# A new order of the steps in a gated recurrence followed by a two-layer MLP

## The chip, the cores and the metric

One core of one Trainium2 chip. The metric is the device time of one execution in microseconds (us). Engines are named as in the profile: PE is TensorE (matmuls), PEld its weight loads, DVE is VectorE, ACT is ScalarE, POOL is GpSimd, SP is SyncE. Every DMA of this kernel is issued by SP ("SPq" in the profile), one after the other.

## The reference

For each of 4 batches and 8 heads (768 tokens, 48 dimensions) a state matrix of 48x48 is carried over the tokens, turned and damped by a complex gate per row; then the outputs of all heads make 3072 rows of 384, which go through a layer of 2048 features with a PReLU.

```python
mag = np.sqrt(a_re * a_re + a_im * a_im)
scale = np.minimum(mag, 0.999) / (mag + 1e-06)
a_re_n, a_im_n = (a_re * scale, a_im * scale)
for t in range(S):
    new_re = ar * S_re - ai * S_im
    new_im = ar * S_im + ai * S_re
    kv = np.einsum('bhd,bhe->bhde', k[:, :, t], v[:, :, t])
    S_re, S_im = (new_re + kv, new_im)
    y[:, :, t] = np.einsum('bhd,bhde->bhe', q[:, :, t], S_re)
...
h = x @ w_in
g = np.maximum(h, 0.0) + alpha * np.minimum(h, 0.0)
return (g @ w_out).astype(np.float32)
```

## The kernel before

**Tiling and stages.** The sequence is cut in chunks of 128 tokens: 4 batches of 6 chunks are 24 *units*. Nine *gate tasks* prepare the gates: three for the first batch (1, 2 and 3 chunks) and two of 3 chunks for each other batch. The work is written as Python generators, one per task; each `yield` ends a *step*, a few instructions on one engine.

- `gates` (L250 on) loads a_re and a_im into a gate buffer (tile gate, two of them in turn; GpSimd's memset L249 clears a last column), normalises the gate on ScalarE and VectorE (L253 to L301), builds products of magnitudes (L318; tile decs, stored by L323) and running products of phases. These are first products of eight neighbours (L338, L340, large ones on VectorE), then of the blocks (the same lines with 128x72 and 128x36 on GpSimd for all batches but the first), a short run over blocks (128x12, 128x6), a correction of the blocks (L396, L399), a renormalisation (L405 to L413), and the final large products on VectorE (L426, L429), which are stored by L421 and L431 (tile phs). ScalarE copies stand between (L366, L368). I call the stretch from the last large product of L340 to L413 GpSimd's chain of the task.
- `loads` brings q and k of a unit (tile KQ, L579, L581), its phases (tile PP, L587, called the rotation load) and its magnitudes (tile T, L594). `half_rows` (L560) copies values into a scratch in DRAM (vsc), `loads_v` brings values (tiles V and VL, L603 to L629).
- `unit` multiplies q and k by the phases (L661, L663), halves the chunk level by level (L717 on VectorE, copies L740 and L756 on ScalarE, sixteen small matmuls L678 on TensorE, masks L699 and L702), transposes k (L785), makes k times v (L797), sums the levels with the values (L817), updates the state (L826, L829 on VectorE) and takes its part of y (L841); ScalarE copies y out (L855), L860 stores it.
- `weights` brings the MLP's weights from 64-bit words to float32: ScalarE L507 to L511, GpSimd L515 (tile top), VectorE L517 and L519. `pieces` issues their loads and the small ones (start, L468; alpha, L471).
- `all_mlp` is the MLP over the finished rows: for each group of up to 256 rows (loaded by L873) and each of 16 blocks of 128 features, three matmuls (L889), ScalarE's relu of the negative part (L896), VectorE's alpha times it plus the input (L898; tile g_sb), and for each 128 rows one matmul into the output (L908), in 16 steps per output tile, copied by L918 and stored by L921.

**What sets the order.** Every instruction stands on its engine in the order in which it is emitted (`tc.manual_schedule()`); engines run their own lists in order, and wait for one another where data or a buffer asks for it. The order of emission is a string, ORDER, of 4292 letters (L30 to L72). Each letter names a task and lets it go one step on:

```python
    LETTERS = "ABCDEFGHIJKLMNOPQRSTUVWXYZabcdefghijklmnopqrstuvwxyz0123456789"
...
    def run(self, order):
        for c in order:
            next(self.tasks[self.LETTERS.index(c)], None)
```

A to I are the nine gate tasks; J is `loads`, K `half_rows`, L `loads_v`, M `pieces`, N and O the two `weights`, P to Z and a to m the 24 units, n `loads_x` and o the MLP. The names DVE, ACT, POOL, PE and DMA in the steps are functions that return nothing; the numbers in them have no effect here.

Of the kernel before, what the change touches and what calls it, by code (L numbers as in the profile page):

```python
# [27 lines left out]


ORDER = (  # L30
    "AAAAAAAAAAAAAAAABJJJJBBAAAAAAAAMMMMMAMAAAAAAAAAAALLLBBNNBBLABLAAALABALAAAANBNABBBBANAABABBANABOOAMBB"
    "OBBOAAAAAAKMAABBBABABABABABBAKKKKAALLKAABABABAABAABNAAAAABANBABALAAABAABNBNOBBBBOOOOBONBMNBNNBBBBNNJ"
    "OBOOOOOBBPBPCBNPCBBBBPCBBBBCCJJJOBBOBBKPPPPBCBBBBBMPNJJLNNBPNNBPBPBPBCNPBNCMBMCPPPPPJPCKKKKKKKKKKKKK"
    "BKBKPBBBMBCPBNOCNBOOBPCMNCLLCCBLPPPPPPPPPPPPPPPPCCMCBCCBKCCCPJOCOCDOJOCNNJCNNNNNCDCCKKKPCPCPPPPPPPPP"
    "CCQCOKOOOCMQCCQLDDDQCCLLLLLLJLLLLLLCLCCCJDJJJJJJJCCNJQQCDNCQCQCDDQQCDCCNNQCDDQQDDQCOCODDCDCDCCCQDDOQ"
    "CQOCQQQCDDDDKOCRQQCRQQQQQQCQQQRRRRQQQQQMnQCNDMCOCOOCDDDMCQCLQCLRCCCCRCRRLLLRCRRRoKJLQOOOOCoRoCoCRRCR"
    "oQQLLLLLoooKLLQLoQQQoQCoCDCooRooQoRRDooCCCCRRRRRRRRRRoCRCoCoCoCDoRQCJJJEooRRODooooNNNNNoEDRooRoRoooo"
    "RDnLLLLooOoOoOoRODLooRoLLLLLLRLLDNRNoLSoooooooooSoRRRRRooJJSooOoooooSoSSDSNDSSSESoooooooRoSNSSoooSDo"
    "ooSSSDJSJJEJJJJJJDoooooDoooEOSSSSooooSDoooSSSSSSooDDDDDDDooETTSSSEESooooSSSSSToSSEEESSooKSSSoSToJTTT"
    "ToooToooSToooTooSLoooToULoDLLoLDTJDDDDDDJTDoToEDTDDoDLDLoDDDDDDooLLLLLoToTLTooooooooooToTTTUTTToTooT"  # L40
    "ooTLJooDTTToooDUUTTTTTToULLLLULEEEEooEoTEoEDDDDDDDDDoDDEooooooUEToooUUUoooooonoUoEooJoUoooooUEUEDTDD"
    "DoTTUUUELEJULoooLLKLLLLKoUoooooDDooDDDJoKDKKoKoooUUUUUUooooDDDTTTTTToUoooUDUUUooooUooDUEDUUUUEUEEEoo"
    "EoEoooooooEoEEUooUooJooEoooUUUUoUUoFUUoooEEEoEoEooooooooooEEoEoEVFooFoJVVooJoFoJJnooooJJJJVJVFoLLooo"
    "oooooVVVFFLoLVoooooooooEEEEEEVoooVVVEEEEEEEEEEELEEEoEJJJooFoWWoEEoEEEVooooVVooVoooWJVVVVFLoooWooLooo"
    "oWVVVVVVWVWWJVoooVFFVooooXVWLoLLLVLLoLooKVKoEEEEWEVVVVVVVVVVVKLLWEEVoKooLLLLLooLXFWLVLLVLVLVVWWWWWoE"
    "EEEELooWooooEoEoEWEEEooJEWWWWWWWWEoooooooooJJEoEJEEEoooEWWWooooWoooWWWWWWWWWXLoooooWoFFFLXoLLXXXoXXo"
    "GLLWWooJoJLLXooXoXWWWWWWooooFoFFXXXXXXFoLooooLooFoXoFoFFFFFFFJJooFooonXoXXXXXGLLLLooFFXooooooXXXXooo"
    "XoXoFYFFFooooFoooFooXoFXXXXXXXXXFFXXXXXJJoYYJoooooLJLJFFFGoooFYLGFFFFFFFFooXoooYYYYYJYoYooXoooooooLo"
    "FFFFFoZZYYYYJooJYoYYZooooooYoooooZGoYYYYYYYYoYFLZZZZZZZFooooLoYYLFFLGFLLLLFLLooooYYoZZoYYYJYYYYJJLJJ"
    "LLGoFZZZLLFLLFLLLLFLooooLFFFFFFFFFFFooZZYooFFFFYZoGGGGFoooFYYYYYYYYZZZoooFooLooooFFFFFFZJFFFZooZZZZZ"  # L50
    "FZFoooooJZooZoZZnZZZZooZZZZZJZaZZLLFFJoLooooZZZJoooFoGaooGooaoaooooGGGLLLLLLLoLLLaaaaoooooooooaJaJaJ"
    "ooooooaGaaaaaoooHoooHoaaooooooGGoooaaGaaaGGaaaGGGooGGGooboaaaKboooooJooooooaooooaHGbGaGJGbJoaaGaabbb"
    "bJoJaaaaaabaaGLLbLLLoGoLGoLLLGaaHooHJooobboGoooooobboooGHobbbHobbooooJbooGHoJoboLHGJoooGbbbGbGbbbbJb"
    "ooocooooGoooJoonbooKoKGccoKKKKKooooooLbcccGcccooooHoooocooGoLLLbGJoJobbbobHbHGHHbbbLbHbGbbbbbLbbboGG"
    "GGGHoHoHoLoooGGGGGoGcGLcoGoGooGGGoGoGoGcGcGcccccLJoJoLooLoooLooooLLLcccLLccLdocoJocGcoGcGccGoocodooc"
    "oHHHddcHcccccccHdLcGGcGKoooLLHHGGHLoHLJLLHHoHooHooHooHdcGcdcdddcHcccooodoooGoooGGGGoGLLdLLLLLoGGGodd"
    "dddoooododoooonooooGooGodGddddooGdoddoooooooGHGddHoodJodHHHoJoJJJHHHJJJooooodooooooddddddddddddddddo"
    "HJeeooooJooooeoooooeoHooHHHHHHHdoLeeeooooooeeeeoefoofoooeeeoeoeooooJJooofLoooooLLooIeeofffeJeeooKooo"
    "oLLLLLLLLLHeeeeeeeeHHHHLooHoHoHoHeHoHeHooeeeeeeeeeeeeeeeJJIJJLLoHHeeHooHHIHfKHHfHHHHHoooHoJHoHooHffJ"
    "ooHoofgIooogoooofffILoHHoofffHoofofHHogHooooLnooooLLLooLoJoLgLHKLffffffffggoLIILggggfoooofKooooKHooL"  # L60
    "HooHgHooooHoHKKoKKHoofoIfKooofffoffffffffffLfJoJoofHfffHoooooHggggggoLLLLLooooIogoogIoooooHggIIIIooo"
    "ooooLgoggLgLLLILoooogggggoooIgILoooogggggggggggggJJJoohJJhhoLLIIJoooJJoggLgoooJooohhILLLoIoInoooLoho"
    "oiiJJhJohoLLJLLLhooooIIooooooooohhohhoIooooooihIhhhoIhhhoIIoIoIhIIIooiooooooooIIIihihhhhhhhooohLILIo"
    "oIooooIohooJJhJooohohoohhhhhIIIiIhIhhLhhhhLLoLooooiiiiooLoooLooooiiiooihohihhihooioioooooooJijJjiiJJ"
    "JIIIIIIIIIIIIIIIIIIIIIIIIIIooiooooIojooiooioioioooooiooooIIijIIIoIIoojjjjjILoIiiIoILoLILoLoLLLiijiij"
    "ioiLLLLLLLjjjLLLiLLoooIIIIIoooiooIIIIIiooooooooooooooijjjojojooLLoooooooojjjjijjjjIIiiiiooojoojooiii"
    "jjjIooJjjjjjjjjjjjjnjoJJJjjjjooooooooooooookooookokokooLoooLJJJJJJJooooooLookkooookkokokookookooookk"
    "kkkkkLLLooooooLLLLLLLoooookkkkoookkkkokooLookookkllokokkJkkkkkkkkkkkkkkololooooooooLLoooLooookLooLLL"
    "LllllllllLoLoooooooooJooooooooooooooooooooooonooooooooooooooooooJoooLLLollloooooooolllloooJooooooJJl"
    "loooooJLlllllllllooooooooololoolllllllllllllllllooooooomooooLoooomoooooooooomooooommmmmmomooooomoooo"  # L70
    "ooooLmmLmLLoooonooLomooooooooomLmmmLooooLLommmmmmmmoooooooomomomLLooooooooooomoooooooLomommmmmmmmmmm"
    "mmmomooooooooooooooooooooooooooooooooooooooooooooooooooooooooooooooooonooooooooooooooooooooooooooooo"  # L72
    "oooooooooooooooooooooooooooooooooooooooooooooooooooooooooooooooooooooooooooooooooooooooooooo")


# [925 lines left out]
```

## Time and profile before

| what | before |
|---|---|
| runs, us | 843.6, 840.4, 843.08 |
| median, us | 843.08 |
| span of the profiled execution, us | 845.2 |
| busy of the costliest line on TensorE (L889), us | 302.0 |
| the next (L908), us | 295.2 |
| costliest lines of VectorE (L717, L898), us | 148.5, 97.4 |
| bytes moved by DMA, MB | 130.91 |

The profile is of one execution, whose own time is its span of 845.2 us; it lies 2.1 us above the median of the runs. Busy time is the time in which an engine executed; the rest is waiting for another engine, a transfer or a buffer. A line of waits names the instruction that waited, who released it, and the time in total, the number of times and the longest. A line of the timeline names the start, the duration, the instruction with its tile shapes, and in brackets how long the engine stood idle before it and who ended that. "VectorE work ahead" of an instruction is the sum of the durations, in the profiled execution, of all VectorE instructions that stand in front of it in an order; it is a place in a list and not a time.

### The profile page before, as it was taken

The numbers are of one execution on the slowest core, as the hardware profiler recorded it, in microseconds if no ns is written. First come the engines' busy times: TensorE is split into PE (matmuls) and PEld (weight loads), VectorE is DVE, ScalarE is ACT, GpSimd is POOL, SyncE is SP. The second block draws the span as 40 slices with busy tenths as digits, with TensorE's granted clock in tenths as the row PEclk, the third lists the DMA queues.
The fourth block names the chain that finished last, engine by engine and source line by source line (L and its number), as shares of the span: only waits on it lengthen the run. The fifth ranks groups of instructions, "written<-read, shape, count | busy, mean of one in ns | idle before, by whom it ended". The sixth has DMA issues, their size and how long they took to land.

```text
span 845.2 us, 26866 instructions
## 1 busy us (share of the span) xinstructions
PE 699.6 (83%) x11488; PEld 529.6 (63%) x11488; DVE 653.3 (77%) x1020; ACT 443.3 (52%) x937; POOL 196.3 (23%) x293
## 2 busy tenths in 40 slices
PE   0002316688899999999999999999999999999998
PEld 0001315566777777767777777777676777777776
DVE  5999998689998999979998997687877656345212
ACT  7679686356745656665565634555444324233211
POOL 6241421126544411450115404300124000000000
PEclk9999997879999999999999999999999999999999
DMA  8496987675469677736965467747644482231100
GB/s 240 142 270 172 281 198 207 186 203 123 118 201 255 143 182 223 182 88 172 264 166 138 134 178 181 201 107 192 159 136 106 115 204 64 69 80 38 37 29 9
DMA packets 194174, 130.91 MB, mean 155 GB/s; under 512 B 74120, under 2 KB 185864, under 8 KB 194056
## 3 DMA queue, kind: packets, MB, share of 16 engines
q1 hardware_dynamic: 194056, 129.20, 59.2%
q8 instruction: 90, 1.47, 0.8%
q14 instruction: 28, 0.23, 0.1%
HBM read 100.82 MB, written 35.71 MB: 162 GB/s over the span
## 4 chain that ended last, share of the span: by engine, by line
PE 63%; DVE 17%; DMA 6%; issue 6%; ACT 5%; SPq 2%; POOL 0%; DVEq 0%; ACTq 0%; POOLq 0%
PE ps_o L908 25%; PE ps_h L889 25%; PE ps_lv L678 4%; DVE KQ L717 4%; PE ps_y L817 3%; PE ps_kv L797 2%; PE ps_y L841 2%; DVE gate L338 2%; DMA PP<-phs 2%; DMA phs<-gate 1%; DMA g_sb<-in_w_in_dram 1%; PE ps_kt L785 1%; DVE gate L426 1%; SPq L626 1%; DVE gate L340 1%
## 5 line engine op out<-in xcount | busy, mean ns | idle before, releaser
L889 PE MATMUL ps_h<-xT,w_in_sb 128*128 128x256 f32 (+1 forms) x1344 | 302.0, 356 | 2.9 <-DVE g_sb L898 1.6
L908 PE MATMUL ps_o<-w_out_sb,g_sb 128*128 128x384 f32 x768 | 295.2, 499 | 5.1 <-DVE g_sb L898 4.9
L889 PEld LDWEIGHTS ps_h<-xT,w_in_sb 128*128 128x128 f32 x1344 | 234.3, 193 | 74.1 <-issue 3.6
L898 DVE SCALAR_TENSOR_TENSOR g_sb<-g_sb,al,ps_h 128x256 f32<-128x256 f32 (+1 forms) x224 | 97.4, 437 | 115.5 <-ACT g_sb L896 115.1
L896 ACT ACTIVATE g_sb<-ps_h 128x256 f32<-128x256 f32 (+1 forms) x224 | 79.0, 353 | 204.2 <-PE ps_h L889 202.7
L908 PEld LDWEIGHTS ps_o<-w_out_sb,g_sb 128*128 128x128 f32 x768 | 138.0, 192 | 56.7 <-DVE g_sb L898 6.9
L717 DVE TENSOR_TENSOR KQ<-KQ,T 96x1024 f32<-96x1024 f32 x120 | 148.5, 1239 | 32.1 <-PE ps_lv L678 23.2
L678 PE MATMUL ps_lv<-WQ 96*32 96x32 f32 x2304 | 34.7, 204 | 79.0 <-DVE WQ L661 55.9
L678 PEld LDWEIGHTS ps_lv<-WQ 96*32 96x32 f32 x2304 | 26.6, 116 | 99.7 <-DVE WQ L661 56.1
L740 ACT COPY WQ<-KQ 96x1024 f32<-96x1024 f32 x48 | 50.0, 1041 | 27.8 <-DVE KQ L717 27.7
L338 POOL TENSOR_TENSOR gate<-gate 128x72 f32<-128x72 f32 x42 | 29.6, 704 | 125.6 <-ACT gate L368 122.8
L855 ACT COPY T<-ps_y 48x256 f32<-48x256 f32 x96 | 30.8, 364 | 51.8 <-PE ps_y L841 51.2
L338 DVE TENSOR_TENSOR gate<-gate 128x576 f32<-128x576 f32 (+5 forms) x84 | 50.0, 595 | 1.1
L515 POOL TENSOR_SCALAR top<-top 128x768 f32<-128x768 f32 x16 | 41.5, 2602 | 32.1 <-ACT top L507 32.1
L678 PE MATMUL ps_lv<-KQ,W 96*32 96x32 f32 x1536 | 25.2, 205 | 27.5 <-ACT W L756 23.2
L817 PE MATMUL ps_y<-A,VL 64*48 64x64 f32 x2304 | 42.4, 223 | 4.1 <-DMA VL<-vsc 2.5
L699 ACT ACTIVATE A<-ps_lv,columns 128x64 f32<-128x64 f32 x144 | 36.2, 336 | 17.2 <-PE ps_lv L678 17.1
L426 DVE TENSOR_TENSOR gate<-gate 128x1152 f32<-128x1152 f32 (+2 forms) x36 | 43.6, 1235 | 0.3
L756 ACT COPY W<-KQ 96x512 f32<-96x512 f32 x48 | 30.8, 642 | 23.9 <-DVE KQ L717 21.1
L817 PEld LDWEIGHTS ps_y<-A,VL 64*48 64x48 f32 x2304 | 39.8, 124 | 5.5 <-DMA VL<-vsc 2.7
L678 PEld LDWEIGHTS ps_lv<-KQ,W 96*32 96x32 f32 x1536 | 20.3, 115 | 29.6 <-ACT W L756 24.7
L785 PE MATMUL ps_kt<-ident,KQ 96*128 96x96 f32 x192 | 26.0, 260 | 15.4 <-DVE KQ L717 12.9
(106 smaller groups left out, 912.1 us busy)
## 6 DMA issues: line engine op xcount, KB each, us to landing
T<-decs SPq DMA_DIRECT2D x48, 384.0 KB
PP<-phs SPq DMA_DIRECT2D x24, 387.0 KB
KQ<-in_q_dram SPq DMA_DIRECT2D x48, 192.0 KB
decs<-gate SPq DMA_DIRECT2D x7, 1152.0 KB
phs<-gate SPq DMA_DIRECT2D x14, 576.0 KB
KQ<-in_k_dram SPq DMA_DIRECT2D x40, 192.0 KB
vsc<-in_v_dram SPq DMA_DIRECT2D x48, 144.0 KB
VL<-vsc SPq DMA_DIRECT2D x24, 288.0 KB
```

The costliest lines, as they stand in the source:

```text
L338: on(4 * k).tensor_tensor(out=m, in0=w[:, 1::-1].unsqueeze(2).to_broadcast([P, 2, 2, k]), in1=pairs_of(u), op=ALU.mult)
L426: TT(out=m[:, a], in0=U5[:, 1 + a], in1=turned(off3, o)[:, a].unsqueeze(1).unsqueeze(3).to_broadcast([P, L // 2, nb, 2]), op=ALU.mult)
L515: nc.gpsimd.tensor_scalar(out=top, in0=top, scalar1=F64_SMALL, scalar2=None, op0=ALU.max)
L678: nc.tensor.matmul(t[64 * i + j:64 * i + j + HC // 2, p], lhsT=keys(n, g), rhs=queries(n, g), start=True, stop=True)
L699: nc.scalar.activation(a[:, :, cols], t[:, :, at:at + name], AF.Copy, scale=s)
L717: nc.vector.tensor_tensor(out=x, in0=x if x0 is None else x0, in1=m, op=ALU.mult)
L740: nc.scalar.copy(z.rearrange("p i n t -> p i (n t)").rearrange("p i (m h) -> p m i h", h=h), bass.AP(tensor=KQ.tensor, offset=KQ.offset + ...
L817: nc.tensor.matmul(o, lhsT=Vp[h][64 * i:64 * i + 64, s, e_ * D:(e_ + 1) * D], rhs=a, start=False, stop=False)
L889: nc.tensor.matmul(p, lhsT=w_in_sb[:, f // 2, kk, f % 2 * P:(f % 2 + 1) * P], rhs=x_of[m][:, kk], start=(kk == 0), stop=(kk == NK - 1))
L896: nc.scalar.activation(gt, p, AF.Relu, scale=-1.0)
L898: nc.vector.scalar_tensor_tensor(out=gt, in0=gt, scalar=al_1[:, f:f + 1], in1=p, op0=ALU.mult, op1=ALU.add)
L908: nc.tensor.matmul(sums[0], lhsT=gt[:, c * P:(c + 1) * P], rhs=w_out_sb[:, f], start=(f == 0), stop=(f == NF - 1))
```

## The change

ORDER is another string with the same letters: each letter occurs as often as before, and so every task goes through the same steps, with the same instructions, shapes, engines and buffers. Only how the tasks are interleaved differs, from the 17th letter on. The heads of both strings, and the rest left out:

```diff
 ORDER = (
-    "AAAAAAAAAAAAAAAABJJJJBBAAAAAAAAMMMMMAMAAAAAAAAAAALLLBBNNBBLABLAAALABALAAAANBNABBBBANAABABBANABOOAMBB"
-    "OBBOAAAAAAKMAABBBABABABABABBAKKKKAALLKAABABABAABAABNAAAAABANBABALAAABAABNBNOBBBBOOOOBONBMNBNNBBBBNNJ"
...
+ORDER = (
+    "AAAAAAAAAAAAAAAAAAAAAAAAAAAMBMAMAJJBJJMBAAAAABAABALAAALAAAALABABAKKAKMKABKAAAMAAAAAAAAAAALABALAAAAAA"
...
```

Where some letters stand in the two strings (count of letters from 0; o is the MLP):

| letter | task | first, before | first, after | last, before | last, after |
|---|---|---|---|---|---|
| A | gate task, first chunk of batch 0 | 0 | 0 | 170 | 141 |
| B | gate task, chunks 1 and 2 of batch 0 | 16 | 28 | 355 | 261 |
| C | gate task, chunks 3 to 5 of batch 0 | 212 | 196 | 667 | 617 |
| D | gate task, first half of batch 1 | 366 | 299 | 1188 | 1150 |
| E | gate task, second half of batch 1 | 671 | 714 | 1555 | 1632 |
| I | gate task, second half of batch 3 | 2783 | 2674 | 3603 | 3524 |
| P | first unit | 209 | 191 | 399 | 503 |
| Q | second unit | 402 | 311 | 666 | 637 |
| X | ninth unit | 1425 | 1535 | 1790 | 1779 |
| b | thirteenth unit | 2156 | 2076 | 2396 | 2415 |
| j | twenty-first unit | 3393 | 3386 | 3628 | 3690 |
| m | last unit | 3955 | 3833 | 4104 | 4139 |
| o | the MLP | 580 | 529 | 4291 | 4291 |

More of the change, by code (lines that the diff above doesn't have):

```diff
@@ L30 @@
 ORDER = (
-    "AAAAAAAAAAAAAAAABJJJJBBAAAAAAAAMMMMMAMAAAAAAAAAAALLLBBNNBBLABLAAALABALAAAANBNABBBBANAABABBANABOOAMBB"
-    "OBBOAAAAAAKMAABBBABABABABABBAKKKKAALLKAABABABAABAABNAAAAABANBABALAAABAABNBNOBBBBOOOOBONBMNBNNBBBBNNJ"
-    "OBOOOOOBBPBPCBNPCBBBBPCBBBBCCJJJOBBOBBKPPPPBCBBBBBMPNJJLNNBPNNBPBPBPBCNPBNCMBMCPPPPPJPCKKKKKKKKKKKKK"
-    "BKBKPBBBMBCPBNOCNBOOBPCMNCLLCCBLPPPPPPPPPPPPPPPPCCMCBCCBKCCCPJOCOCDOJOCNNJCNNNNNCDCCKKKPCPCPPPPPPPPP"
-    "CCQCOKOOOCMQCCQLDDDQCCLLLLLLJLLLLLLCLCCCJDJJJJJJJCCNJQQCDNCQCQCDDQQCDCCNNQCDDQQDDQCOCODDCDCDCCCQDDOQ"
@@ L36 @@
[L36 to L70, printed above, removed]
@@ L71 @@
-    "ooooLmmLmLLoooonooLomooooooooomLmmmLooooLLommmmmmmmoooooooomomomLLooooooooooomoooooooLomommmmmmmmmmm"
-    "mmmomooooooooooooooooooooooooooooooooooooooooooooooooooooooooooooooooonooooooooooooooooooooooooooooo"
+    "AAAAAAAAAAAAAAAAAAAAAAAAAAAMBMAMAJJBJJMBAAAAABAABALAAALAAAALABABAKKAKMKABKAAAMAAAAAAAAAAALABALAAAAAA"
+    "BAABABBBABBBBAAAAOBBAABAABABOBNABAABABABAALBBJBNBKNBBBBNBBBBBBNOBBOBBNBBBBNBBNBBOBBBBOBNBLNPBBBBCBBC"
+    "BKNCBBPPBJBLPKJBBBBBCCBNBBBCCBBMBBMKJBBBMPBBBBNBCKBKBLPCNNPKLBJPCKPOPCOPPPOCCCCCOKJPPCCCLOCCJJCPCLJD"
@@ new lines @@
+    "DCNOJPCOPPCQJPDCJMMPCDPQLNCDOCLPPPKPCCKNNJCKPNPNCPPPPPOPKDPPPONPCPCQKCCOMQCCKPDCCNDNOPOCQCMDPOCQQPOM"
+    "CQCQPPOCDQQJCPCOCNQNCOQLLLLLLOQQCCOQOONCCDCCQQCCOJOCCKKQKLDRLQCQQCMDNQLQCPKQPDQDCDCLPPNCMLCDNNNLCQQL"
+    "NCDPCQQQQLMQJQCODQQJCNnQNCCCOoDLNROJCCCoQCLCoCQLLOOQONOOLMOCLCQCKCCRQoCCCRDoQLoRoooCCJooKCCoooooCoND"
+    "DCooooNoMoRoQRDoLCQOooooooRRoRLooQQQoQooRJooooNoONRoRoNNRoRoooNLoJooDRRoooOJJRLoooLoLLOJooooRSRNNJJR"
+    "oRooooRRoROoSJEDooooRoNRORoSREROONooRooSSSSnRSRRRRSRLOLRSDDDDESRoLDDoRooooRDoLLRoLLLLLRSoJRSRSJRoooo"
@@ new lines @@
+    "RSRooooSLoSoDSRoLLSooSDLSEoSSooSoooSDJoooJDoooDoDoSoSDoSSooTDSDEoSoTJDoKDKoToSSDoJDooSDEoDoSSSoTTDoE"
+    "SoJJSoDLLJLDToTooSTTEooTooDETSoSooSKKKoooToSDoEKSoSSoESoKoToEooTooSKKEETJoooLLoEoLooooJonTTLTDLoLooo"
+    "JoDDDDDDDDDDDDDDUToDoLDDLDooLoLDJDoUTDoTooDDDoJoEooToDDEooooDDoTDoDoDDoTTooEETDooTLDoDDTTTDoUoUooooD"
+    "TooooToTETDoDoDTTToLooDDLDoooEoooLLTLEUUoEUUoTooELDoLUEoUUTULLoLEJoTooToFETToUFEUoEUoJoEoUoUEUToUTEo"
+    "oooooToUoUoUTUEUoUooVLLUUUoEUooTooULUVoVUJoFUFUUEUJUULEFoVJUEUEULUUUJVooLUoEooVVEoUVUJJVoVooJEoEoooo"
@@ new lines @@
+    "oVoKoVVooVooVonLoVFEFLVooVoVLLooJVJooLELFEEJVooLELELWoEooLVWoKEEEoVWEVooEEFFEEooooVooVEVEWVoVoooLEoW"
+    "WWVVWooKoVoVKFoWoFVoVVVVVWFWVWLWVoVWVWLWFLoVVVJJVEJoEEKLVVoFWWoLEFoEoEEJEWEEVoFoEEEoooEEoEELWWEVoEWL"
+    "oEoLLFLWoooLWooLFoLoEWWoLWJWEooEooEXEEooWoooWJEEEoXJEFJEoJEEKoooXoEWoWoXFFooEoWWWoEFWFFoWXKLXFLoooFo"
+    "oEXoLooLLXXWoXWoLooXooooooFWXWoLELFLLLFoWFJWWLXWLoWXWXLXXoWXooWFoJXooooooooXFnFXXYFoJXXJoJXoXFJooXoX"
+    "FoYooFXoXoXoXooooooFoGGXXFXYXXXXJFFXXXoYLXXYXXFYYoJoFJYXoXoFoooooFYYZLoYGooooFoXooooooLYZJGYLJYGLLLL"
@@ new lines @@
+    "LYYZYYooYoooZooooooZJLoZLFFFFFFFFFFFFZJFFLFYFZLFFFLFJYoYYYGZYoZYoooYYYooYKFZJoooYoGoYYYGYYYGYYJFFFFY"
+    "FFFFLFoFFLYYZYZZLFFYYYYYYooFLFLJJoGJaoLGoFLFooZoFFoooFLLoFaZLooooooooooFZLLLLnZGGFZFooaooKFooooaoooo"
+    "GZJZJFZZaZZZaooFFFooZoFooZooooZoFoaZoZooZJZaaZZZJKZZaZZZZZZZZZaZZGooooooLLJGbJGooooooaaaaooGoooGoooo"
+    "oaoaoGHaooooaobooboGLHbLLboGLGoboLGoJoooooLoLoaLaabbbaooaLooLaaGboGoKbKbaooaaoooGaoGoaooLaaGHGbGGaab"
+    "aabaaGboaaaLLoaaaGbKooooGJJJoHbGoGbGaobGooHabooGooJooJGooJoGGGbbGbbobooHoLoJnoHHoJoooccooocooboobbbH"
@@ new lines @@
+    "HLoboooHoLoobooLobooLLLGGGbLoLLGoLGGGGLbGGGcGHHHbbHGbGbbLbbGGocGccbGGGGGGbcJcbHocGbboGoobGGoGcHoocoo"
+    "JoJbGGcHHLbcccHbooLoooHooLLdJdJcoooKoGooooooocGooodGocHGGGGodGooGooHGHoJodLGdGdcJccHcoocLHLLLLLcocGc"
+    "GGdooodoooodGLccLooJcoooocGoHocdGcHcHdcccccdHHHcLdHccdcccoGLooooGoodooLJdoooGHLoooLcoLGoooHLLLLLLdLc"
+    "odoooGoooooooooocoHcHdJddddoLdHooooHooHooooodoHJooodJeeooddodHoodooedddHHdIddddJeHJedJIdHKLeeedHdooL"
+    "LLHnHHHJddLLLdLoooeHeLLLHLdHHHooIooeoooHHLHHHHHHHooodeeeeeoeoedooooJJJooeooooeJeooIeoeeooIooooIoeeeI"
@@ new lines @@
+    "eoofHeooKooooeoefofLeoooHHHoooooefeeeefIIeefHeeIJeIfIHeIIeeJeeoooeJLoHoeLIofJfoLIooHHHLLJoIoHJoIoffI"
+    "LJgHHHLooooooooLoLfooooHogooHIoffffgIKnfIfooooHHLHHoLLooooogooooHoofLoHIHoooggffoffofoofooggoLJggooo"
+    "oHfHHHHooHHoofHooKoJHooooIooIooooHfffIoofoofoooIooHgfofffffgfLfIIIIKIgfgffffffggooIgogooLIoogoooIooo"
+    "ooIogIgKLgJfJIIIILIogofLooLIgggggIIIIILIIIoIJIIIoooooooooooogoKIgIoIooohJhhLoooIoLooooooLooJhooooIoh"
+    "LggoooLLhggJggJgJoIhhggLhgLggghhhghIgooooIooooooIoooooooooLJoLLIoighigooohhhJJhoohoooLLoohnhioiJKoIo"
@@ new lines @@
+    "oooohLJhIiLLhKohhhohhIKIIioooIIIIIooILIKIIIohiiiooJLhooohhLoooohJLiohhhihhhiihJoihhohijhhijIhhhiohhJ"
+    "IIooioooooooIooIJIIIIoooooooooIoooIIoooooLiLIJLLLLLLLLLLjoJoooooojooiojijIijiiojioiiojiIioIiooLijooj"
+    "oooooLiIiiiiijioiiLiLLjjIjoiiLJjijiioooooiiioooooojooooooooooooooooojJjjJJJnJooojjjjjjjoLLLoLookoooj"
+    "kjkokojoLojooooooooooooLLoLoLLjjjjjjjjjkkjjLjjLLLLjLLooLLooooLLoooooooojoooooooooJoooooojJjoJkoJookJ"
+    "ooJoJJkkokoooooooklklkolkokooklkooookooooolkkkLkLLlllkkkoJokkooooookoooookoooooooooooooookookokkklkk"
@@ L73 @@
+    "kLllllkkkollklkkJkJkookLoookkoolnmoLoooooooLoJJoooooooooooolooooooooLLooolLLLooooomooomLoomoooLLolLL"
+    "lmmllllolmooolomolmmmlloooooooooooooooooooooooooolooooooooolllmllllmllmlllLlLloolLoolomomommoLollmno"
+    "oooooooLooooommmoLmmooooooomooooooooooooooooooooLooLooooommmLmoooooooooooooooLLoooooLooooooooooooooo"
+    "ooooooooooooLmoomooomoooommmmmmmmmmmmmmmnooooooooooooooooooooooooooooooooooooooooooooooooooooooooooo"
     "oooooooooooooooooooooooooooooooooooooooooooooooooooooooooooooooooooooooooooooooooooooooooooo")
```

## The prediction

> **What bounds the kernel now.** I read the page's busy line first, then its 40 slices, then busy time by stretch, then the waits of VectorE, then single instructions of GpSimd. Columns of the first fence: busy time, share of the span; then a digit for each slice of 21.1 us.
>
> ```profile
> span 845.2 us, 26866 instructions
> PE 699.6 (83%) x11488; PEld 529.6 (63%) x11488; DVE 653.3 (77%) x1020; ACT 443.3 (52%) x937; POOL 196.3 (23%) x293
> PE   0002316688899999999999999999999999999998
> DVE  5999998689998999979998997687877656345212
> PEclk9999997879999999999999999999999999999999
> PE 63%; DVE 17%; DMA 6%; issue 6%; ACT 5%; SPq 2%; POOL 0%; DVEq 0%; ACTq 0%; POOLq 0%
> ```
>
> The two engines take turns: VectorE is nearly full for some 230 us while TensorE waits for it, then TensorE is full to the end (63% of the chain in the last line). Cutting the span there:
>
> ```profile
> core 0: us, PE busy (x) PEld busy (x) DVE busy (x) ACT busy (x) POOL busy (x), PEclk, DMA share, GB/s
> 0.00:229.30 229.30, 97.47 (x2240) 77.22 (x2240) 202.29 (x380) 158.18 (x267) 78.33 (x90) 0.95 0.72 195
> 229.30:845.20 615.90, 602.12 (x9248) 452.34 (x9248) 451.06 (x641) 285.17 (x671) 117.95 (x203) 1.00 0.56 140
> ```
>
> At 229.3 us VectorE finishes the g_sb tile (L898) for the 28th output matmul (L908). It was busy 202.3 us of these 229.3 and stood 27.0 us; TensorE has 615.9 us behind it. So the span is **VectorE work ordered ahead of a hand-off + VectorE's idle time before it + TensorE work ordered behind it**, for the hand-off where that is largest. An order can change all three terms, and no instruction's duration. I lay every instruction at its duration in the profiled execution in each order's sequence (TensorE by mean spacing: L889 0.454 us for 256 columns and 0.239 for 128, L908 0.672, sixteen L678 0.418, thirty-two L797 0.969).
>
> Part of the idle time has a name:
>
> ```profile
> DVE g_sb L898 <- ACT g_sb L896: 6.5, 6, 2.5
> DVE gate L259 <- ACT gate L257: 5.4, 1, 5.4
> DVE top L517 <- POOL gate L249: 4.6, 1, 4.6
> DVE gate L269 <- ACT gate L267: 2.4, 1, 2.4
> ```
>
> (waits of VectorE in 0 to 230 us: total, times, longest.) Third line: VectorE stands 4.6 us in L517 because GpSimd's L515 ahead of it stands behind a small memset (L249) of the fifth gate task, which waits until the third task's store (L431) has left that buffer.
>
> **The change, part by part.** Counts by engine are equal in both orders: VectorE 1020, ScalarE 937, GpSimd 296, SyncE 731, TensorE 5984 instructions as written (the page's larger count has each float32 matmul twice, and not all of GpSimd's records). Nothing is added or removed; so all of the cost is in the three terms.
>
> *The work ahead and behind.* Same hand-offs in both orders (us; VectorE ahead + TensorE behind):
>
> - 28th output matmul: before 202.2 + 618.8 = 821.0, after 189.2 + 623.9 = 813.1
> - 47th output matmul: before 241.4 + 573.9 = 815.3, after 243.9 + 573.1 = 817.0
> - state update to y (L829 to L841) of the ninth unit: before 304.2 + 506.5 = 810.7, after 307.6 + 507.8 = 815.4
> - 144th output matmul: before 402.9 + 395.9 = 798.8, after 415.6 + 391.2 = 806.8
>
> Before has one peak and then 10 to 20 us to spare; after has no peak but a plateau of 812 to 817 from the 40th to about the 220th us of its TensorE work, falling to 793 at 400. The peak falls by 4.0 us. But a small wait of VectorE after 230 us, which in the old order costs nothing, is paid in full on a plateau. This decides my number.
>
> *Idle time up to the first hand-off.* 27.0 us in before. L517's 4.6 us go: the memset now stands behind nearly all the L515s, and the last L515's result is wanted at 150.4 us of VectorE work where the store is ready at 132.8, which is 18 us later. What is late next is the fourth gate task, D. Its small products run on GpSimd (these rows are of before; last field: idle before, and who ended it):
>
> ```profile
> 207.92 0.32 POOL L338 TENSOR_TENSOR gate<-gate 128x72 f32<-128x72 f32 x1
> 208.65 1.19 POOL L338 TENSOR_TENSOR gate<-gate 128x72 f32<-128x72 f32 x1
> 224.11 0.89 POOL L396 TENSOR_TENSOR gate<-gate,runs 128x252 f32<-128x252 f32 x1 [4.13 <-ACT runs L368]
> 236.14 4.41 POOL L318 TENSOR_TENSOR gate<-gate 128x72 f32<-128x72 f32 x1 [0.25 <-DVE gate L318]
> ```
>
> From VectorE's last big product (L340) to GpSimd's last step (L411 and ScalarE's L413) this chain took 40.0 us for D, 37.3 for E, 33.3 for F, 28.1 for I. VectorE's work between that product and its first L426, which needs the chain's end, was 40.5, 36.0, 29.5 and 21.3 us; in the new order it is 27.3, 29.7, 29.0 and 31.9. So D and E lose their room. If the chains keep their lengths, VectorE stalls 40.0 - 27.3 = 12.7 us for D, 37.3 - 29.7 = 7.6 for E and 4.3 for F. If they run at the sum of their own pieces with no queueing (28 to 34 us, I's 28.1 being a whole one), it is 0 to 6 for D, and 0 to 4 for E. I take 2.5, 2 and 1: part of the old lengths was queueing behind other ScalarE work (4.13 us in the third row), which a chain with room to spare can afford and which the new order need not repeat.
>
> [...] The same 128x72 product takes 0.32 and 1.19 us, and L318's 4.41 us while VectorE runs L426 with both inputs in SBUF. [...]
>
> *TensorE's clock.* In the page's slices 7 and 8 the granted clock is below full; in detail 23.9 us between 138 and 190 us are at half clock. The new order wants 38.9 us of TensorE work done where the old one wanted 35.6 (at the end of the third unit): 3.3 us more, so 0 to 3.3 us of lateness; I take 1.
>
> *Start of the run.* The alpha load (L471, 3.4 us of issue) and the start load (L468) now stand on SyncE ahead of the second gate task's a_im load, and the small value copies (L560) are spread out rather than in runs. VectorE had waits only for ScalarE's own chain there (second and fourth line of the waits). I take 0, bounds -2 to 3.4.
>
> So in place of the 27.0: 27.0 - 4.6 + 2.5 + 1 = 25.9.
>
> *Idle time beyond.* Before's VectorE stood 4.1 us more up to the 47th output matmul, 3.5 more up to the ninth unit, 8.4 more up to the 144th. TensorE was full meanwhile, so some of these waits are VectorE waiting for TensorE, which a later VectorE does not have. I take half of each: 2.0, 1.8, 4.2; bounds none and all.
>
> *The sums.* Before's own sums miss its span slightly, as the mean spacings do (202.2 + 27.0 + 618.8 = 848.0 against 845.2: -2.8; -1.2 at the 47th; 0 at the ninth unit); I carry these corrections.
>
> - 28th (D's chain ends behind it): 189.2 + 23.4 + 623.9 - 2.8 = 833.7
> - 47th: 243.9 + 27.9 + 573.1 - 1.2 = 843.7
> - ninth unit: 307.6 + 29.7 + 2 (chain E) + 507.8 = **847.1**
> - 144th: 415.6 + 29.7 + 2 + 1 + 4.2 + 391.2 = 843.7
>
> The span comes out at 847.1, 1.9 above before's. The median of the three runs shown (843.08) is 2.1 under before's span (845.2), so the time is 847.1 - 2.1 = **845.0**. Half a per cent of 843.08, 4.2 us, is about what a measurement of this kernel can tell from no change: 838.9 to 847.3 counts as the same.
>
> *Later parts.* The work of TensorE behind the last unit falls from 46.1 to 36.6 us; TensorE is full there in both, so nothing. Unit b's rotation load (L587) has 7.3 us of room behind F's store, against 4.9 + 5.2 = 10.1 for the landing of the store and of the load: about 3 us of VectorE, where the sums have over 20 to spare: nothing.
>
> **The rivals.**
>
> 1. *No new stalls: faster.* The chains fit and VectorE's waits after 230 us were all for TensorE. For it: VectorE operations at 100 to 500 us of its work with under 1.5 us of room behind their producer number 39 in the old order and 16 in the new. Then the ninth unit gives 307.6 + 22.4 + 507.8 = 837.8 with nothing else late; with 1 to 3 us of waits 839 to 841, so 836 to 839 as a time.
>
> 2. *GpSimd's chains keep their lengths: slower.* D's and E's 12.7 and 7.6 us in place of my 2.5 and 2 make 847.1 + 15.8 = 862.9, so 861 as a time; half of it 853. It decides once D's chain is longer than 27.3 us by more than 6. For it: the rows above; against it: the shortest chain, 28.1.
>
> 3. *SyncE's queue: slower.* Transfers are issued in order. The first sixteen value loads (L626, L629) of unit j now stand behind the last store (L431) of gate task I, which waits for VectorE's L429, and behind loads of unit k. In before they left ahead of it:
>
> ```profile
> 652.67 6.34 SPq L626 DMA_DIRECT2D VL<-in_v_dram  x9
> 672.42 0.38 SPq L431 DMA_DIRECT2D phs<-gate  x1
> ```
>
> Sixteen and the loads between need about 18 us from that store to the last landing, and TensorE wants it (L817) at about 680 us. The store comes at 662 by the VectorE work ahead of it: 0 to 1 us. If it comes at before's 672, TensorE stands 10 to 11 us with the MLP's matmuls queued behind: 845 + 11 = 856. It decides from 663 us on.
>
> **How the numbers follow.** Forecast (841 to 849) 0.36, of it 0.28 within the bound and 0.08 slower; first rival 0.26 (0.22 faster, 0.04 within); second 0.16 (0.14 slower, 0.02 within); third 0.12 (0.10 slower, 0.02 within); something else, above all in the first 150 us where the new sequence differs most, 0.10 (0.04, 0.02, 0.04). Together: faster 0.26, same 0.38, slower 0.36. The range: below, the first rival's 836 with the start's 2 us, **834**; above, the second rival's 861 with the rest of the clock and start bounds, **864**. The forecast's own range, 841 to 849, holds the largest single share.
>
> **What would show it.** Right: TensorE is not full until about 340 us, VectorE over 90% busy to there, and the first hand-off is no longer the last wait; L517's 4.6 us are gone. Wrong for the chains: waits of L426 on GpSimd (L411, L413) near 227 and 300 us of 0 (first rival) or of 8 to 13 us (second). Wrong for the queue: a wait of TensorE's L817 for VL near 680 us. Wrong altogether: VectorE's idle time before 150 us other than before's by over 4 us.

## The result, and the profile after

The changed kernel takes 884.07 us in the median (878.29 to 891.38, 4 runs) against 842.18 us for the kernel before on the same chip; the ratio is 1.052, 95% interval 1.0458 to 1.0582: some 42 us **slower**. The forecast was 845.0, no change, and its range ended at 864.

The page of the kernel after, first its span, busy times and slices, then the chain:

```profile
span 882.1 us, 26858 instructions
PE 713.2 (81%) x11488; PEld 540.4 (61%) x11488; DVE 655.9 (74%) x1020; ACT 440.2 (50%) x937; POOL 190.0 (22%) x293
PE   0001427799899998998999889999999999999998
DVE  5999999989889898888898975998568536353212
PEclk9999997989899999999999998999999999999999
PE 58%; DVE 13%; DMA 8%; issue 6%; ACT 5%; POOL 5%; SPq 5%; DVEq 0%; ACTq 0%; POOLq 0%
```

TensorE's digits are no longer an unbroken 9 from 230 us on: five slices between 220 and 530 us show an 8, and the clock shows an 8 in two slices, at 220 and at 530 us. Cut at the place where before's span was cut (columns: length of the stretch; busy time and instructions of TensorE, its weight loads, VectorE, ScalarE and GpSimd; granted clock; DMA share; GB/s):

```profile
0.00:229.30 229.30, 99.21 (x2038) 78.38 (x2039) 204.62 (x379) 154.24 (x265) 77.07 (x92) 0.95 0.73 198
229.30:882.10 652.80, 613.97 (x9451) 462.00 (x9449) 451.24 (x642) 286.01 (x672) 112.92 (x202) 0.98 0.50 131
```

The first 229 us are slightly better than before's: VectorE did 204.6 us of work in place of 202.3. All of the loss lies behind, in TensorE: 38.8 us idle (652.80 - 613.97) against before's 13.8 (615.90 - 602.12), and it is busy longer, at a mean clock of 0.98 in place of 1.00. What it waited for behind 230 us (total, times, longest; the largest rows), first in the kernel before:

```profile
PE ps_lv L678 <- issue: 4.1, 2, 2.2
PE ps_y L841 <- issue: 1.7, 2, 1.1
PE ps_h L889 <- DVE g_sb L898: 1.6, 2, 0.8
PE ps_h L889 <- issue: 1.2, 1, 1.2
```

and in the kernel after:

```profile
PE ps_lv L678 <- issue: 13.6, 11, 2.0
PE ps_y L817 <- issue: 11.1, 4, 3.6
PE ps_lv L678 <- ACT W L756: 4.8, 3, 2.6
PE ps_y L841 <- issue: 3.3, 2, 1.7
PE ps_o L908 <- DVE g_sb L898: 0.7, 2, 0.4
```

"issue" names no releaser: TensorE stood 28 us for nothing that the profile shows, in the small matmuls of the units (L678, L817, L841). One such place is unit X's, in the timeline of the kernel after (start, duration, instruction, idle time before it):

```profile
343.97 1.15 PE L797 MATMUL ps_kv<-V,T 64*64 64x48 f32 x64
344.94 0.29 PE L808 MATMUL ps_y<-ident,nothing 64*48 64x256 bf16 x4
345.05 1.10 PE L817 MATMUL ps_y<-A,VL 64*48 64x64 f32 x62
349.73 1.22 PE L817 MATMUL ps_y<-A,VL 64*48 64x64 f32 x34 [3.59 <-issue]
```

and the same step in the kernel before:

```profile
336.74 0.29 PE L808 MATMUL ps_y<-ident,nothing 64*48 64x256 bf16 x4
336.84 1.52 PE L817 MATMUL ps_y<-A,VL 64*48 64x64 f32 x96
338.29 1.10 PE L841 MATMUL ps_y<-KQ,St 96*48 96x64 f32 x32
```

The 96 rows of one line ran through in before; in after they stopped behind the 62nd, and the profile names no engine or transfer that they waited for. Three facts point to the supply of instructions. The stops of the kernel after stand in TensorE's list at rows 3258, 3637, 4016, 4650, 5030, 5536, 5917, 6424, 6805 and so on: whole multiples of 126.8 rows apart (379, 379, 634, 380, 506). The page has a queue of its own for them:

```profile
q8 instruction: 90, 1.47, 0.7%
```

90 transfers of 16 KB, for 11488 matmul rows and as many weight loads: one for about 255 instructions, that is 127 rows. And each stop ends 2.2 to 2.6 us behind the start of one of these transfers (at 347.3 us for the stop above). I call such a stretch a *block* and a stop at its end a *block-end stop*. Behind 230 us before has 5 of them over 0.45 us (7.1 us), after 17 (28.0 us). (Stops are counted by their place at a block's end; in some kernels below one of them is put down to an engine by the profile, and this is said there.) A block that lies wholly within a run of small matmuls, without an MLP matmul between, is used up in 1.8 to 4.1 us; most others have several MLP matmuls in them and take 4 to 26 us.

Three of after's blocks, with one to six MLP rows at or near their start, take 1.6 to 4.1 us and end without a stop, so the time of a block alone does not decide. The start of the transfer goes with the stop: with the transfers laid beside the blocks in order, the one that a stop waits for starts 0.6 to 3.3 us behind the first row of the block ahead of the stop, in all 17 cases, and 2.1 to 3.8 us ahead of that row in these three. (In two blocks of small matmuls that end without a stop it starts 1.1 and 1.4 us behind the row; these blocks took 3.4 and 3.9 us.) By and large, the later it starts, the longer the stop: 0.8 to 1.2 us long where the transfer starts 0.6 to 0.7 us behind the row, 3.2 and 3.6 us where it starts 2.7 and 3.3 us behind. What sets the start of a transfer is open.

This the order decides. In before a unit's run is mostly 196 rows; in after, the next unit's L678 steps (64 rows) stand within the run, which has 260. Counted in the two orders with the trace's block ends, 4 whole blocks lie inside such runs behind 230 us in before, and 19 in after. Of before's 4 all end in a stop, and of after's 19 all but two, which follow directly on a block of the other 17. One stop of before stands behind a block with 123 small rows of 127.

### The profile page after: what moved, and what is told of

Read it like the earlier page. It is cut to its first block, busy times and chain, and to the rows that moved or that the text cites. A ratio compares the mean times of both kernels' runs of the same rounds, so it can differ in the third digit from the quotient of the medians.

```text
span 882.1 us, 26858 instructions
## 1 busy us (share of the span) xinstructions
PE 713.2 (81%) x11488; PEld 540.4 (61%) x11488; DVE 655.9 (74%) x1020; ACT 440.2 (50%) x937; POOL 190.0 (22%) x293
## 4 chain that ended last, share of the span: by engine, by line
PE 58%; DVE 13%; DMA 8%; issue 6%; ACT 5%; POOL 5%; SPq 5%; DVEq 0%; ACTq 0%; POOLq 0%
PE ps_h L889 22%; PE ps_o L908 22%; PE ps_lv L678 4%; PE ps_y L817 4%; DVE KQ L717 3%; PE ps_y L841 3%; PE ps_kv L797 2%; DMA T<-decs 2%; SPq L626 2%; DVE gate L426 2%; PE ps_kt L785 1%; DVE gate L338 1%; POOL gate L338 1%; DMA ysc<-T 1%; DMA PP<-phs 1%
## 5 line engine op out<-in xcount | busy, mean ns | idle before, releaser
L908 PE MATMUL ps_o<-w_out_sb,g_sb 128*128 128x384 f32 x768 | 301.0, 507 | 8.2 <-DVE g_sb L898 8.0
L889 PEld LDWEIGHTS ps_h<-xT,w_in_sb 128*128 128x128 f32 x1344 | 238.7, 196 | 74.7 <-issue 4.9
L908 PEld LDWEIGHTS ps_o<-w_out_sb,g_sb 128*128 128x128 f32 x768 | 140.3, 195 | 62.6 <-DVE g_sb L898 12.0
L678 PE MATMUL ps_lv<-WQ 96*32 96x32 f32 x2304 | 35.6, 204 | 76.1 <-DVE WQ L661 50.5
L678 PEld LDWEIGHTS ps_lv<-WQ 96*32 96x32 f32 x2304 | 27.2, 116 | 92.4 <-DVE WQ L661 50.5
L817 PE MATMUL ps_y<-A,VL 64*48 64x64 f32 x2304 | 45.2, 230 | 19.6 <-issue 19.2
L338 POOL TENSOR_TENSOR gate<-gate 128x72 f32<-128x72 f32 x42 | 26.7, 636 | 139.2 <-ACT gate L368 106.7
L817 PEld LDWEIGHTS ps_y<-A,VL 64*48 64x48 f32 x2304 | 42.0, 130 | 21.1 <-issue 20.3
L678 PE MATMUL ps_lv<-KQ,W 96*32 96x32 f32 x1536 | 25.9, 204 | 32.9 <-ACT W L756 23.7
L756 ACT COPY W<-KQ 96x512 f32<-96x512 f32 x48 | 30.7, 640 | 38.7 <-DVE KQ L717 29.1
L699 ACT ACTIVATE A<-ps_lv,columns 128x64 f32<-128x64 f32 x144 | 38.2, 332 | 11.4 <-PE ps_lv L678 11.4
L426 DVE TENSOR_TENSOR gate<-gate 128x1152 f32<-128x1152 f32 (+2 forms) x36 | 43.3, 1226 | 0.7 <-POOL gate L411 0.7
L678 PEld LDWEIGHTS ps_lv<-KQ,W 96*32 96x32 f32 x1536 | 20.5, 115 | 36.4 <-ACT W L756 24.8
L785 PE MATMUL ps_kt<-ident,KQ 96*128 96x96 f32 x192 | 26.0, 261 | 17.1 <-ACT T L788 12.5
```

Source lines behind the costliest of these rows:

```text
L338: on(4 * k).tensor_tensor(out=m, in0=w[:, 1::-1].unsqueeze(2).to_broadcast([P, 2, 2, k]), in1=pairs_of(u), op=ALU.mult)
L426: TT(out=m[:, a], in0=U5[:, 1 + a], in1=turned(off3, o)[:, a].unsqueeze(1).unsqueeze(3).to_broadcast([P, L // 2, nb, 2]), op=ALU.mult)
L678: nc.tensor.matmul(t[64 * i + j:64 * i + j + HC // 2, p], lhsT=keys(n, g), rhs=queries(n, g), start=True, stop=True)
L699: nc.scalar.activation(a[:, :, cols], t[:, :, at:at + name], AF.Copy, scale=s)
L817: nc.tensor.matmul(o, lhsT=Vp[h][64 * i:64 * i + 64, s, e_ * D:(e_ + 1) * D], rhs=a, start=False, stop=False)
L889: nc.tensor.matmul(p, lhsT=w_in_sb[:, f // 2, kk, f % 2 * P:(f % 2 + 1) * P], rhs=x_of[m][:, kk], start=(kk == 0), stop=(kk == NK - 1))
```

## The experiments

**Theory** (block theory): block-end stops, and the half clock behind them, make the difference. (Of the 30.9 us at half clock behind 230 us in after, 27.3 begin within 1.2 us of the end of a block-end stop, and 3.4 behind a wait of 2.63 us for a W copy.) **Rivals**: VectorE's hand-offs are late on the plateau, as the forecast had it; or a stop belongs to its step's own transfers or buffers.

*Moving the block ends, not the order.* 32 matmuls that nobody reads, at the head of TensorE's list, where it is idle, move every block end by 64 rows:

```diff
-        plan.run(ORDER)
+        idle = ps.tile([P, HP, D2], F32, tag="misc", name="ps_idle"); [nc.tensor.matmul(idle[:, 0], lhsT=ident, rhs=ident[:, :D2], start=True, stop=True) for _ in range(32)]; plan.run(ORDER)
```

> The kernel after, with 32 added float32 matmuls (64 rows of the trace, with their weight loads) into an unused PSUM tile at the head of TensorE's list, where TensorE is idle; their result is read by nobody. Block theory: every gap that has no other engine as its releaser moves by half a block against the steps, so that counted in the kernel's own rows the gaps stand 64 rows earlier or 63 later than in the kernel after, still whole multiples of 126.8 rows apart; the number stays at 14 to 20 and the span at 872 to 892. Rival (each gap is a wait of the step it stands in, for a transfer or a PSUM buffer): the gaps stay at the same steps.

Measured: 880.77 us, ratio 1.0445 (1.0383 to 1.0506), 17 block-end stops, 27.1 us. In the program's own rows they now stand at 3574, 4081, 4587, 5473, 5981: 64 rows before a multiple, so at other steps than in after, at the same place of the instruction stream. The rival that they belong to a step falls.

The same with 28 matmuls in the kernel before, whose order stays as it is:

> The kernel before, order untouched, with 28 added float32 matmuls (56 rows with their weight loads) into an unused PSUM tile at the head of TensorE's list, read by nobody. They move the block ends by 56 rows against the steps. Block theory: 17 whole blocks then lie inside runs of small matmuls behind 230 us, where the kernel before has 4; 13 more gaps at after's 1.55 us of gap and 0.9 us of clock each: 20 to 32 us slower, 862 to 876, though no step of the program moves. Rival (the order costs through VectorE, ScalarE, GpSimd or SyncE): within 4 us of before.

Measured: 876.71 us, ratio 1.0375 (1.0326 to 1.0425); 18 block-end stops, 32.8 us (one of 1.1 us is put down to VectorE by the profile). TensorE's waits behind 230 us:

```profile
PE ps_y L841 <- issue: 12.9, 7, 4.6
PE ps_y L817 <- issue: 9.3, 6, 2.8
PE ps_o L908 <- issue: 5.1, 2, 2.6
PE ps_lv L678 <- issue: 4.4, 2, 3.0
```

The fast kernel becomes nearly as slow as the changed one with no step of it moved. Its control, 58 matmuls:

> Control for the shift: the kernel before with 58 added matmuls (116 rows) at the same place. Block theory: 3 whole blocks inside runs, as many as the kernel before's 4: within 5 us of before, 838 to 848. Rival (added matmuls at the head cost time by themselves, through the clock or a delay of the first unit): slower by about twice what the 28 matmuls cost.

Measured: ratio 0.9972 (0.9933 to 1.0011), 5 block-end stops, 6.4 us:

```profile
PE ps_y L817 <- issue: 5.5, 4, 2.3
PE ps_h L889 <- DVE g_sb L898: 1.8, 2, 1.0
PE ps_h L889 <- issue: 1.3, 2, 0.9
```

The added matmuls cost nothing by themselves. Nor does the lower mean clock of the kernels with added matmuls: it is 0.916 in this control, 0.912 in the slow kernel with 28, and 0.986 in before. 13 more stops cost 0.0375 x 843 = 32 us: 2.4 us each, of it some 2 us of standing ((32.8 - 7.1) / 13) and the rest, by the block theory, half clock: an estimate. The new order, with 39 and with 46 added matmuls:

> The kernel after, order untouched, with 39 added matmuls (78 rows) at the head of TensorE's list: 15 whole blocks inside runs behind 230 us in place of 19. Block theory at 2.4 us each: 10 us faster than after, 868 to 878. Otherwise: the same as after.

> The same with 46 added matmuls (92 rows): 22 whole blocks. Block theory: 7 us slower than after and 17 slower than with 78 rows, 884 to 894. Otherwise: the same as after.

Measured: 1.0369 (1.0332 to 1.0406) with 14 stops, 1.0588 (1.0554 to 1.0623) with 20 (one of them, of 1.65 us, is put down to ScalarE by the profile, and a wait of L797 for ScalarE of 1.6 us stands in the kernel with 39 too; without it they are 19). Waits of TensorE behind 230 us, first with 39, then with 46 added:

```profile
PE ps_lv L678 <- issue: 10.2, 4, 4.3
PE ps_y L841 <- issue: 7.7, 5, 3.0
PE ps_y L817 <- issue: 7.4, 5, 2.5
```

```profile
PE ps_y L841 <- issue: 14.1, 8, 3.1
PE ps_lv L678 <- issue: 11.9, 6, 3.3
PE ps_y L817 <- issue: 7.7, 6, 2.0
```

Seven more matmuls, 18 us: 3.1 us for each of the 6 stops, or 3.7 for each of 5. At 2.4 to 3.1 us, after's 12 stops more than before's are worth an estimated 12 x 2.4 = 29 to 12 x 3.1 = 37 us of the 0.052 x 843 = 44 us.

*Curing the long runs by moving the MLP.* The order around unit X, in the first experiment and in the fifth (letters as in ORDER, the moved o's being steps of the MLP):

```diff
-XXFXYXXXXJFFXXXoYLXXYXXFYYoJoFJYXoXoFooooo
+XooXFXYXXooXXJFFXXXYLXXYXXFYYJFJYXXoFooooo
```

> The kernel after, with 18 of its long runs of small matmuls broken: behind each unit's k times v matmuls (L797) the MLP's next matmul, and behind its last value matmuls (L817) the next two (with the MLP's ScalarE and VectorE steps between them) are emitted earlier than in the kernel after; all else stands as there. No run of matmuls outside the MLP is then longer than 168 rows of the trace. Block theory (TensorE stops where its instruction stream passes a block boundary, when the block before was used up in under some 2.6 us by small matmuls alone): gaps over 0.45 us behind 230 us fall from 33.9 us to under 12, the time at half clock there from 30.9 us to under 7, span 843 to 853. Rival (late VectorE hand-offs on the plateau, as forecast): TensorE's idle time only moves to waits for VectorE; span 875 to 888.

Measured: 881.32 us, ratio 1.0463 (1.0396 to 1.0531): missed, and in the range that the rival gave. The block-end stops fell to 7 (11.7 us), but other waits rose from 5.8 to 12.9 us, and some 32 more changes between MLP and small matmuls cost an estimated 8 us (0.24 us each, as the fourth experiment shows below).

```diff
-XXFXYXXXXJFFXXXoYLXXYXXFYYoJoFJYXoXoFooooo
+XoooooooXFXYXXXXJFFXXXooo
...
```

> The kernel after, with breaks only where a whole block of TensorE's instructions (126.8 rows of the trace, at the phase that the gaps of the kernel after show) lies inside a run of small matmuls: 19 places behind 230 us. In each the next four MLP matmuls (some 2 us), with the MLP's ScalarE and VectorE steps between them, are emitted from behind the run into the middle of that block; all else stands as in the kernel after. Block theory: the 17 gaps at block ends (26 us) and the half clock behind them (15 us of loss) go; 19 more changes between MLP and small matmuls cost some 0.28 us each (what the first experiment's rows show), 5 us; gaps of other kinds stay (some 6 us): span 843 to 854. Rival (late VectorE hand-offs, as forecast): the places of the breaks are nothing special; span above 868, like the first experiment.

Measured: 881.37 us, ratio 1.0424 (1.0381 to 1.0467): missed too, again in the rival's range. The stops did go, 28.0 to 3.5 us, and these waits came (with the rest of the stops in the last row):

```profile
PE ps_lv L678 <- ACT W L756: 11.8, 9, 3.7
PE ps_h L889 <- DVE g_sb L898: 5.9, 8, 2.5
PE ps_y L817 <- DMA VL<-vsc: 5.0, 2, 3.8
PE ps_y L817 <- issue: 2.8, 2, 1.4
```

Waits other than block-end stops rose from 5.8 to 26.1 us. With 24.5 us less of stops, some 5 us less lost at half clock (21.6 us in place of 30.9) and some 4 us for 18 more changes, that leaves a gain of about 5 us, and the trace's span is 4.1 us shorter than after's. The last but one is a wait for values as in the third rival of the prediction, though not its wait: it is at 649 us, in the nineteenth unit and not in the twenty-first, come up once TensorE was in another place. Is this the cure or the order? The same cure in the shifted kernel before:

> The kernel before with the 28 added matmuls (block ends moved by 56 rows, as in the sixth experiment) and with breaks of four MLP matmuls in the 17 whole blocks that then lie inside runs of small matmuls. It asks why the same cure brought nothing in the order after. If the cure works where the order has room elsewhere: the gaps at block ends go and 16 more changes cost 4.5 us: 846 to 856. If breaks by themselves bring waits for data (the MLP matmuls moved into a run are missing behind it as cover): 866 to 880, as in the fifth experiment.

Measured: 866.1 us, ratio 1.0203 (1.0176 to 1.0231) against 1.0375 without: block-end stops 32.8 to 8.8 us, others 0 to 10.1. Half is regained. So moving MLP matmuls into a run brings waits for data of its own (they are missing behind the run, where they had covered VectorE's and ScalarE's next steps: this is argued, not shown), and more of them in the new order.

*Is it VectorE?* The additions L429 of the later gate tasks are left out:

```diff
-            TT(out=by_place(p), in0=m[:, 0], in1=m[:, 1], op=ALU.add)
+            TT(out=by_place(p), in0=m[:, 0], in1=m[:, 1], op=ALU.add) if b == 0 else None
```

> The kernel after without the same 12 additions (left out). If only TensorE's block ends hold it: within 5 us of 882. If the gaps count because VectorE has no room left (a lost 2 us of TensorE delays VectorE, which cannot catch up): 8 to 16 us faster, 868 to 876.

> The fifth experiment's kernel (order after with breaks) without the additions L429 of the six gate tasks of batches 1 to 3: 12 instructions of 1.35 us, 16.2 us of VectorE's work; this part of the gates is left out. If VectorE's lateness is what holds that kernel (the plateau of the forecast): 9 to 16 us faster than it, 865 to 872. If TensorE's own losses or ScalarE's and SyncE's lists hold it: within 4 us of 881.

> Control: the kernel before without the same 12 additions (left out). TensorE is full from 229 us, and all but the first gate tasks' additions lie behind that: within 4 us of before by every theory, 841 to 848; more than that would mean that the old order, too, waits for VectorE behind 229 us.

Measured: 1.0443 (1.0419 to 1.0467) for the kernel after, 1.0372 (1.0353 to 1.0392) for the fifth experiment's, 0.9988 (0.9962 to 1.0015) for before. 16.2 us less work on VectorE change none of them beyond the spread: the intervals of the first two overlap, though barely, with those of the kernels they were made from (1.0458 to 1.0582, 1.0381 to 1.0467), and the gains in the middle, some 6 and 4 us, stay under the 9 to 16 us that VectorE's lateness would give. The plateau as the forecast priced it, VectorE's lateness paid in full, falls; that a few us hang on VectorE is not excluded.

*Other changes of order.* Merging runs in before, and breaking its runs:

```diff
-XoFXXXXXXXXXFFXXXXXJJoYYJoooooLJLJFFFGoooFYLGFFFFFFFFooXoooYYY
+XoFXXXXXXXXXFFXXXXXJJYYJLJLJFFFGFYLGFFFFFFFFXYYooooooooooooooY
```

> The kernel before, with the MLP's steps between a unit's run and the next 64 rows of small matmuls moved behind these in 11 places (4 to 15 of TensorE's MLP matmuls each), so that runs of 200 become runs of 264, as the kernel after has them; all else stands as before. Block theory: a gap of 0.6 to 3.6 us in nearly each of the 11, some with half clock behind them, as in after (1.6 us of gap and 0.9 us of clock each): 11 to 30 us slower, 854 to 873. Rival (late VectorE): within 4 us of before.

Measured: 900.05 us, ratio 1.0665 (1.0607 to 1.0724), more than either theory gave. Stops without a releaser rose to 9 (8.4 us), but L678, now too early, also waits 26.3 us for the W copies (L756), and 54.6 us are at half clock behind 230 us: two causes in one edit, so it tells little.

> The kernel before, with its long runs (196 to 232 rows) broken in 16 places as in the first experiment. Block theory: before's gaps without a releaser (8.1 us at 223, 369, 538, 625, 655 and 756 us) mostly go: 835 to 842. Rival (late VectorE): MLP matmuls come a little earlier, VectorE's hand-offs are what counts: 841 to 846, no difference that can be measured.

Measured: 852.71 us, ratio 1.0105 (1.0073 to 1.0137): slower, missed. The stops fell to 3 (3.0 us), but other waits rose from 2.3 to 7.5 us, and TensorE is busy 706.7 us in place of 699.6, for 30 more changes between MLP and small matmuls: 0.24 us each, if all of it is theirs.

> The kernel before, with breaks of four MLP matmuls only in its 4 whole blocks inside runs of small matmuls behind 230 us. Block theory: four gaps (1.95, 0.6, 2.2 and 1.1 us) go, four more changes between MLP and small matmuls cost 1.1 us: 3 to 6 us faster, 836 to 841. Rival (late VectorE): no difference that can be measured.

Measured: ratio 1.0001 (0.9971 to 1.0032): missed, since the interval allows a gain of 2.4 us at most. Two block-end stops of 5 are left (2.7 us of 7.1), but other waits are 1.2 us longer, 3.4 us at half clock are new, and 3 more changes have their price.

> The kernel after, with the next unit's 32 small matmuls (two L678 steps, 64 rows) that stand inside or right behind 16 of its long runs moved out of them, behind the next two MLP matmuls, together with that unit's own steps up to there. Runs of 260 and 228 rows become 196 and 164, as in the kernel before; 8 whole blocks are left in them in place of 19. Block theory: 11 fewer at 2.4 us, 16 more changes at 0.28 us: 22 us faster than after, 855 to 867. If something else in the new order holds it: within 6 us of 882.

> The last kernel with 30 added matmuls at the head of TensorE's list, so that 12 or 13 whole blocks lie in runs in place of 8; no step moves. Block theory: 10 to 12 us slower than it. Otherwise: the same time.

Measured: 1.0398 (1.0351 to 1.0444) and 1.0356 (1.0295 to 1.0417). The first gained about 1 per cent, less than expected, with 10 block-end stops left (17.5 us) and 8.8 us of other waits; the second, expected slower, was not: it has 12 stops but shorter ones (14.6 us; one of 0.6 us is put down to VectorE) and 3.4 us at half clock in place of 17.1. The count of whole blocks gives neither the length of a stop nor all of them: in the first experiment all 7 stand behind blocks with two to four MLP rows in the middle, and with 46 added matmuls one stands behind a block with 22, whose transfer started 9.1 us behind its first row.

No version here beats the kernel before by more than its interval.

## Why the prediction was wrong, point by point

**What bounds the kernel** was read rightly: VectorE first, then TensorE to the end. **The first hand-off** came nearly as worked out: the 28th output matmul started at 216.1 us in place of 229.3, 13 us earlier, where the sum had 189.2 + 23.4 = 212.6. L517's 4.6 us are gone, and VectorE's idle time before 150 us is 14.6 us in place of 17.5.

**The step that failed** is "an order can change all three terms, and no instruction's duration", with TensorE's work laid at before's mean spacing. Behind the 28th output matmul the sum had 623.9 - 2.8 = 621.1 us of TensorE work; it took 666.0. Behind the 47th 604.5 in place of 571.9, behind the ninth unit 530.3 in place of 507.8, behind the 144th 405.8 in place of 391.2: the loss grows evenly over the rest of the run. The sum had no term for stops that name no releaser, though TensorE's waits in before show them, and it took the clock behind 230 us as full. Of these 45 us, 20.9 are block-end stops more than before's, up to 15.5 are clock (30.9 us at half clock behind 230 us, none in before; after the stop at 346.1 to 349.7 us the clock is half for 6.8 us), and 3.5 are other waits over 0.45 us; a wait of 3.1 us for VectorE at 221 us and 3.4 us of clock lost behind it lie between the hand-off and 230 us.

The stops and the clock behind them have these sizes: of after's 19 blocks of small matmuls alone behind 230 us, 17 end in a stop, of 0.8 to 3.6 us (up to 4.6 us in the kernel before with 28 added matmuls), and none of its blocks with MLP matmuls ends in one over 0.45 us. The clock stood at half from 295.1 us on, behind a stop of 1.66 us at 293.1 us, and from 755.9 us on, behind one of 1.64 us at 753.8 us, for 3.4 us each time.

**Idle time of VectorE and GpSimd's chains** (second rival; in the sum at 2.5, 2 and 1): the kernel after shows one wait of L426 for L411, of 0.7 us. By the prediction's own measure D's and E's chains took 31.1 and 34.0 us, in place of 40.0 and 37.3, so the room of 27.3 and 29.7 us of VectorE work, with VectorE's own waits, was enough but for these 0.7 us. Whether VectorE's products beside them lengthened these chains was not measured. **SyncE's queue** (third rival): the wait for the twenty-first unit's values did not come; its first L817 (at 710.5 us) did not wait. Another unit's L817 waited 0.4 us for values in after, and 3.8 us in the fifth experiment, so value loads are near the edge. **The first rival**, no new stalls, was right on VectorE's side but for the 3.1 us at 221 us. The plateau's sign, VectorE over 90% busy to 340 us, did not show: it was busy 91% of 200 to 250 us, 88% of 250 to 300 and 85% of 300 to 400.

**Left open.** The new order without its additional block-end stops was not reached. From after's ratio less 12 stops at 2.4 to 3.1 us, it would be at 1.008 to 1.017 of before, 849 to 857 us: an estimate from the runs above. The same working from the kernel with 39 added matmuls (1.0369, 9 stops more than before) gives 1.004 to 1.011. Whether the rest is half clock, the order's other waits, a few us of VectorE or the spread is not settled. Every edit that took stops away by moving steps gave much of the gain back in other waits and in changes between MLP and small matmuls; what the new order takes without its stops is therefore worked out from prices, and not shown.

## What to carry to other kernels

In this kernel TensorE's list came in 90 transfers of 16 KB, one for about 255 instructions, and each further stop at a block's end cost some 2.4 to 3.1 us (an estimate from the runs with 28, 39 and 46 added matmuls). So where an engine is full, look at the profile's instruction queue, count the instructions in a row that are done in tens of nanoseconds (here 127 rows of small matmuls in 1.8 to 4.1 us, 14 to 32 ns each), and ask how often a whole block falls into such a run. A wait for "issue" on the bounding engine in the profile before (here 4.1 us in L678) is the sign to follow, even when it is small: the block-end stops, 7.1 us in before, were 28.0 us with the new order and 32.8 us with 28 added matmuls. The kernel before is fast at its own phase of the blocks, and 3.75% slower with the block ends moved by 56 rows: before a change of order is judged, shift the phase and measure both again.

## What the runs showed of the hardware that was not expected

28 float32 matmuls of no use, added where TensorE was idle, make the kernel before 3.75% slower (3.26 to 4.25); 58 make it no different. A change between the MLP's 128x128 matmuls and the units' small ones, there and back, takes some 0.24 us of TensorE (an estimate from 30 more of them in the fourth experiment). In after, half clock follows stops as short as 1.64 us, but not each: behind the one of 2.12 us at 494.6 us the clock stayed full.
